# A fused attention and spectral-mixing kernel: TensorE gathers four chunks that transfers used to rearrange, and the last loop's accumulators hold the same half of two blocks

## The chip, the cores and the metric

The kernel runs on one core of one Trainium2 chip. The metric is the device time in microseconds (us) of one execution, as the median of several. Before and after, and every experiment beside the kernel before, ran on the same chip. The profiled execution has its own clock: its span, from the first to the last instruction, is about 2 us shorter than the time of the run (457.1 of 458.82 us before).

Names used below: TensorE does matrix products (PE in the profile, PEld its weight loads), VectorE (DVE) and ScalarE (ACT) do elementwise work, and SyncE (SP) here only issues transfers. SBUF is the on-chip memory; the kernel's tiles in it have up to 128 partitions. The accumulators that TensorE's products go to here are in PSUM.

## The reference

The input of the second part is the output of a causal attention, laid out as `x` with 8 batches, 576 positions and 512 channels. The change touches only the second part:

```python
# x: (8, 576, 512); w_r, w_i: (64, 512, 512); w_ch: (512, 512)      -- attention cut
X = np.fft.rfft(x, axis=1)
Xr, Xi = np.real(X[:, :64]), np.imag(X[:, :64])
Yr = einsum('bmd,mde->bme', Xr, w_r) - einsum('bmd,mde->bme', Xi, w_i)
Yi = einsum('bmd,mde->bme', Xr, w_i) + einsum('bmd,mde->bme', Xi, w_r)
y = np.fft.irfft(Yr + 1j * Yi on the first 64 modes, n=576, axis=1)
u = x + y
return u + np.maximum(u @ w_ch, 0.0)                                 # (8, 576, 512) float32
```

The weights `w_r` and `w_i` are 134 MB and are read once.

## The kernel before

The 64 modes are worked in 8 chunks of 8 modes. When the last quarter of a chunk's weights has been used, its spectrum `y` stands with mode, part and batch mixed on the partitions. The inverse transform needs modes on the partitions and batches beside each other. So each chunk is **spread**: a transfer from SBUF to SBUF rearranges 128 KB into `yv`. For the first four chunks, the product of `y` with `w_ch` is done straight from a transposed copy, eight batches one after another:

```python
def spread(c, which, rows):
    nc.sync.dma_start(out=yv[16 * c : 16 * c + 16, :, which, :], in_=rows)
# at the end of a chunk's last quarter, for every chunk c:
    spread(c, 0, yb)

def first_times_wch(b):                       # called for b in 0..7, after chunk 3
    vp = auxpool.tile([P, DM], FP32, name="v_ps", tag="aux")
    n = 2 * MC * NY                           # 64 rows
    for dt in range(DT):
        nc.tensor.matmul(
            vp[:n], yt_first[:, dt].rearrange("p c (x b) -> p (c x) b", b=B)[:, :, b],
            wch_sb[:, dt, :], start=(dt == 0), stop=(dt == DT - 1),
        )
    nc.vector.tensor_copy(out=yv[:n, b, 1, :], in_=vp[:n])
```

After the last chunk comes a loop over 18 pairs of blocks of positions. A block has 128 positions. Batches end in a short block of 64, and two of the pairs hold those. The product `x @ w_ch` of 16 pairs was made earlier, while weights were loading, and kept in SBUF in one of two **ways**. "e" keeps it as a rounded half-precision part and what the rounding lost, which a VectorE subtraction makes; TensorE puts it back into an accumulator with four products by the identity. "s" keeps it in full precision, and ScalarE copies it back. This putting back is called **seeding**:

```python
ways = dict(zip(kept, "esesessesesseses"))

def seed(i):
    ...
    if ways.get(i) == "s":
        nc.scalar.copy(out=zs[i], in_=z1s[i])
    elif ways.get(i) == "e":
        for x in range(2):
            for y in range(2):
                nc.tensor.matmul(zs[i][:, x, :], ident16h, z1s[i][:, y, x, :],
                                 start=(y == 0), stop=False, skip_group_check=True)

def start_u(i):                                # puts x into the accumulator of u = x + y
    ...
    for x, (b, T) in enumerate(pairs[i]):
        for r, bb, ident in parts(b, T):
            nc.tensor.matmul(us[i][x][r, :]..., ident, x_all[: r.stop - r.start, :, bb, T, :],
                             start=True, stop=False, ...)

def finish(i):
    ...
    for x, (b, T) in enumerate(pairs[i]):
        o = rs[i][:, x, :]
        nc.vector.tensor_tensor(out=o, in0=us[i][x], in1=o, op=ALU.add)     # u + relu(z)
        for r, bb, _ in parts(b, T):
            nc.sync.dma_start(out=out[bb, bass.ds(T * P, r.stop - r.start), :], in_=rs[i][r, x, :])

for i in range(NPRE, len(pairs)):
    pre(i)                                     # seed "e", then the inverse transform into z
    start_u(i)
    add_y(us[i], i, 0)                         # the inverse transform into u
    if ways.get(i + 1) == "s":
        seed(i + 1)
    relu(i, 2 if i == last else 1)             # ScalarE, z -> result tile
    finish(i)                                  # VectorE add, write
```

An accumulator `us[i][x]` or `zs[i][:, x]` holds one whole block, so a write of 256 KB goes to 128 consecutive rows of the output.

The softmax here doesn't subtract the row's maximum and nothing guards it: scores larger than these inputs give would overflow.

Of the kernel before, what the change touches and what calls it, by code (L numbers as in the profile page):

```python
# [9 lines left out]
FP32 = mybir.dt.float32  # L10
# [3 lines left out]
ALU = mybir.AluOpType  # L14
# [4 lines left out]
def kernel(  # L19
# [11 lines left out]
    nc = tc.nc  # L31
    B, H, S, D = q.shape
    NM = moe_w_r.shape[0]
    DM = H * D
# [40 lines left out]
    G_np[:, 0, :S] = cmv[:, None] * np.cos(ang.T)  # L75
    G_np[:, 1, :S] = -(cmv[:, None] * np.sin(ang.T))
    G_np = G_np.reshape(P, SP).astype(np.float16)

    d_ident16h = nc.inline_tensor(ident_np.astype(np.float16), name="c_ident16h").ap()
    d_ident32 = nc.inline_tensor(ident_np, name="c_ident32").ap()  # L80
# [349 lines left out]
    def modes(g, c, meanwhile=None):  # L430


        ps = auxpool.tile([P, DM], FP32, name="yp", tag="aux")
        for x in range(4):
            ri, par = divmod(x, 2)
            cols = xs[g % 2].rearrange("p k r b m -> p (k r b) m")
            c0 = (48, 16)[ri] - 16 * par
            if meanwhile and x in meanwhile:
                meanwhile[x]()
            for cg in range(4):  # L440
                nc.tensor.matmul(  # L441
                    ps[32 * cg : 32 * cg + 32, :],
                    cols[:, c0 : c0 + 32, c * MC + 2 * cg + par],
                    wt[(g, c, ri, par)][:, cg, :],
                    start=(x == 0), stop=(x == 3),
                    tile_position=(0, 32 * cg), skip_group_check=True,
                )
        if g == 0:
            nc.vector.tensor_copy(out=y_acc[:, c, :], in_=ps)
        elif g < NG - 1:  # L450
            nc.vector.tensor_tensor(out=y_acc[:, c, :], in0=ps, in1=y_acc[:, c, :], op=ALU.add)
        else:
            yb = spool.tile([P, DM], FP16, name="y_sb", tag="y")
            for cols in halves if c == NCK - 1 else [slice(0, DM)]:
                nc.vector.tensor_tensor(
                    out=yb[:, cols], in0=ps[:, cols], in1=y_acc[:, c, cols], op=ALU.add
                )
            spread(c, 0, yb)
            return yb

    halves = [slice(i * DM // 2, (i + 1) * DM // 2) for i in range(2)]
# [1 line left out]
    def spread(c, which, rows):  # L463

        nc.sync.dma_start(out=yv[16 * c : 16 * c + 16, :, which, :], in_=rows)
# [8 lines left out]
    kept = list(range(NPRE, len(pairs)))  # L474


    ways = dict(zip(kept, "esesessesesseses"))

    first_pairs = [i for i in kept[1:] if pairs[i][0][1] < NF and pairs[i][0][0] <= 4][:6]
    z1s, xts1 = {}, {}  # L480

    def kept_place(i, t):

        if ways[i] == "e":
            z1s[i] = t.bitcast(FP16).rearrange("p (y x e) -> p y x e", y=2, x=2)
        else:
            z1s[i] = t.bitcast(FP32).rearrange("p (x e) -> p x e", x=2)

    def keep_product(i, xx, z):
        if ways[i] != "e":  # L490
            nc.scalar.copy(out=z1s[i][:, xx], in_=z)
            return
        nc.scalar.copy(out=z1s[i][:, 0, xx], in_=z)
        nc.vector.tensor_tensor(out=z1s[i][:, 1, xx], in0=z, in1=z1s[i][:, 0, xx], op=ALU.subtract)
# [84 lines left out]
    def parts(b, T):  # L579
# [2 lines left out]
            return [(slice(0, P), b, ident16h)]  # L582
        return [(slice(NL * i, NL * i + NL), b + i, ident16h[:NL, :NL]) for i in range(2)]

    def x_transposed(i):
        xts[i] = xt_sb[len(xts) % 2]
        for x, (b, T) in enumerate(pairs[i]):
            ps = upool.tile([P, DT, P], FP32, name="xt_ps", tag="u")
            for rows, bb, ident in parts(b, T):
                for dt in range(DT):  # L590
                    nc.tensor.matmul(
                        ps[:, dt, rows], x_all[: rows.stop - rows.start, dt, bb, T, :],
                        ident, start=True, stop=True, skip_group_check=True,
                    )
            nc.vector.tensor_copy(out=xts[i][:, x], in_=ps)  # L595

    def x_times_wch(i, last):
        zs[i] = z = zpool.tile([P, 2, DM], FP32, name="z_ps", tag="z")
# [38 lines left out]
        spread(c, 1, vb)  # L637
        return vb

    def first_times_wch(b):  # L640
        vp = auxpool.tile([P, DM], FP32, name="v_ps", tag="aux")
        n = 2 * MC * NY
        for dt in range(DT):
            nc.tensor.matmul(
                vp[:n], yt_first[:, dt].rearrange("p c (x b) -> p (c x) b", b=B)[:, :, b],
                wch_sb[:, dt, :], start=(dt == 0), stop=(dt == DT - 1),
            )
        nc.vector.tensor_copy(out=yv[:n, b, 1, :], in_=vp[:n])


    ahead = []
# [19 lines left out]
    def add_y(dst, i, which, rows=slice(0, P), start=False):  # L671
# [4 lines that stand above are left out]
                    dst[x][r, :], G_sb[rows, bass.ds(T * P, r.stop - r.start)],  # L676
                    yv[rows, bb, which, :], start=start, stop=True, skip_group_check=True,
                    tile_position=(0, r.start),
                )
# [9 lines left out]
    def start_u(i):  # L689
        pool, tag = ((upool, "u"), (auxpool, "aux"))[i % 2]  # L690
        us[i] = [pool.tile([P, DM], FP32, name="u_ps", tag=tag) for x in range(2)]
        for x, (b, T) in enumerate(pairs[i]):
            for r, bb, ident in parts(b, T):
                nc.tensor.matmul(  # L694
                    us[i][x][r, :].rearrange("p (g d) -> p g d", d=P), ident,
                    x_all[: r.stop - r.start, :, bb, T, :],
                    start=True, stop=False, skip_group_check=True, tile_position=(0, r.start),
                )

    def result(i):  # L700

        if i % 2 == 0 or i == len(pairs) - 1:
            return finpool.tile([P, 4 * DM], BF16, name="r_sb", tag="r", bufs=3).bitcast(FP32).rearrange(
                "p (x e) -> p x e", x=2
            )
        t = wpool.tile([P, WM, DM], BF16, name="r_w", tag="w")
        return t.rearrange("p m e -> p (m e)").bitcast(FP32).rearrange("p (x e) -> p x e", x=2)

    def relu(i, parts_=1):
        rs[i] = result(i)  # L710
        for x in range(parts_):
            n = 2 // parts_
            nc.scalar.activation(
                out=rs[i][:, n * x : n * x + n], in_=zs[i][:, n * x : n * x + n], func=ACTF.Relu
            )

    def finish(i):
        if ways.get(i) == "v":
            rs[i] = result(i)
        for x, (b, T) in enumerate(pairs[i]):  # L720
            o = rs[i][:, x, :]
            if ways.get(i) == "v":
                nc.vector.tensor_tensor(out=o, in0=zs[i][:, x, :], in1=z1s[i][:, x, :], op=ALU.add)
                nc.vector.scalar_tensor_tensor(
                    out=o, in0=o, scalar=0.0, in1=us[i][x], op0=ALU.max, op1=ALU.add
                )
            else:
                nc.vector.tensor_tensor(out=o, in0=us[i][x], in1=o, op=ALU.add)
            for r, bb, _ in parts(b, T):
                nc.sync.dma_start(  # L730
                    out=out[bb, bass.ds(T * P, r.stop - r.start), :], in_=rs[i][r, x, :]
                )

    def z_of(i):
        return [zs[i][:, x, :] for x in range(2)]

    for c in range(NCK - 2):
        yb = modes(NG - 1, c)
        for x in range(TAKE[c] - 1):
            work()  # L740
        yt = y_transposed(yb, c)
        if TAKE[c]:
            work()
        if c >= NY:
            y_times_wch(c, yt)
        elif c == NY - 1:
            for b in range(B):
                first_times_wch(b)
    work()
    assert not order_z and not ahead  # L750
    c = NCK - 2
# [46 lines left out]


    def seed(i):  # L800
        if ways.get(i) in ("e", "s"):
            zs[i] = zpool.tile([P, 2, DM], FP32, name="z_ps", tag="z")
        if ways.get(i) == "s":
            nc.scalar.copy(out=zs[i], in_=z1s[i])
        elif ways.get(i) == "e":
            for x in range(2):
                for y in range(2):
                    nc.tensor.matmul(
                        zs[i][:, x, :], ident16h, z1s[i][:, y, x, :],
                        start=(y == 0), stop=False, skip_group_check=True,  # L810
                    )

    def pre(i):

        if ways[i] == "e":
            seed(i)
        elif ways[i] == "v":
            zs[i] = zpool.tile([P, 2, DM], FP32, name="z_ps", tag="z")
        add_y(z_of(i), i, 1, start=ways[i] == "v")

    if ways[NPRE] == "s":
        seed(NPRE)
# [3 lines left out]
    for i in range(NPRE, len(pairs)):  # L826
        pre(i)
        start_u(i)
        add_y(us[i], i, 0)
        if ways.get(i + 1) == "s":  # L830
            seed(i + 1)
        if ways[i] != "v":
            relu(i, 2 if i == last else 1)
        finish(i)


# [28 lines left out]
```

## Time and profile before

| | before |
|---|---|
| median of three runs | 459.39 us (458.98 to 459.42) |
| span of the profiled run | 457.1 us |
| last weight lands | about 417.7 us |
| last loop starts | 423.9 us |
| last output data | 455.3 us |

Four readings: the first two come from the page's list of transfers (out and in, engine, count, size of one, median us from issue to landing) and from the view of the output tensor (issue durations on SyncE as minimum, median and maximum in ns, then first and last start):

```profile
out_dram<-r_sb SPq DMA_DIRECT2D x16, 256.0 KB, 2.3
```

```profile
L730 SPq DMA_DIRECT2D out_dram<-r_sb x24: 332/346/597, 423.3 to 453.5; - x24
```

A write of 256 KB lands 2.3 us after its issue, and SyncE needs about a third of a microsecond to issue it. The timeline of TensorE where the first four chunks are multiplied by `w_ch` (start, duration, engine, line, operation, tiles, shape, count, and in brackets the idle time before it and what ended it):

```profile
377.18 9.01 PE L644 MATMUL v_ps<-wch_sb,yt_first 128*64 128x512 f16 x32 [0.68 <-ACT yt_first L626]
```

This is the work that the gather replaces: 9.0 us without a pause. The next lines are stretches of 4 us around it. Their columns are the stretch, its length, busy time and count of PE, PEld, DVE, ACT and POOL, the granted TensorE clock, the mean DMA share and GB/s:

```profile
378.00:382.00 4.00, 4.00 (x13) 2.45 (x12) 1.66 (x3) 0.00 (x0) 0.94 (x2) 0.67 1.23 217
382.00:386.00 4.00, 4.00 (x19) 3.28 (x17) 3.12 (x5) 0.00 (x0) 0.74 (x1) 1.00 1.24 206
```

The fourth is TensorE's timeline again, at its last group of weight products:

```profile
418.11 0.45 PE L441 MATMUL yp<-w_sb,xs 128*32 128x512 bf16 x4 [0.68 <-DMA w_sb<-in_moe_w_i_dram]
```

It idles 0.68 us until the last weights have landed.

### The profile page before, as it was taken

How to read it: one execution, taken by the hardware profiler on the slowest of the kernel's cores; microseconds unless marked ns; L12 is line 12 of the kernel's file. 1: busy time of each engine (PE TensorE's matmuls, PEld its weight loads, DVE VectorE, ACT ScalarE, POOL GpSimd, SP SyncE). 2: the span in 40 equal slices, each digit the busy share in tenths (PEclk: the TensorE clock that was granted, in tenths of full speed). 3: DMA queues.
4: the chain of work that ended last, by engine and by line, in shares of the span. 5: the costliest groups of instructions: out<-in, count | busy, mean ns of one | idle time of the engine just before them, and what ended most of it. 6: DMA issues, size and time to landing. Idle time of an engine off the chain costs nothing.

```text
span 457.1 us, 10262 instructions
## 1 busy us (share of the span) xinstructions
PE 339.1 (74%) x4177; PEld 217.2 (48%) x4209; DVE 237.3 (52%) x528; ACT 219.1 (48%) x382; POOL 182.9 (40%) x269
## 2 busy tenths in 40 slices
PE   1779968966562979936587766779967769797995
PEld 1556646644341656614355544446643326343432
DVE  7777645653242556624345544466656425442675
ACT  1587856554241747723445345446622220221895
POOL 6755555544345555344454444355423223200000
PEclk9999999998586889957778799899999778999999
DMA  9999999999999999999999999999999999995688
GB/s 177 201 203 203 202 201 204 202 204 204 204 204 201 202 202 202 204 205 204 199 192 205 204 204 204 204 203 202 207 206 212 210 210 210 214 214 105 235 285 319
DMA packets 109375, 94.54 MB, mean 207 GB/s; under 512 B 28480, under 2 KB 104512, under 8 KB 109328
## 3 DMA queue, kind: packets, MB, share of 16 engines
q0 software_dynamic: 98960, 81.81, 113.0%
q1 hardware_dynamic: 10368, 12.07, 8.5%
q8 instruction: 33, 0.54, 0.4%
q14 instruction: 14, 0.11, 0.1%
HBM read 164.56 MB, written 9.44 MB: 381 GB/s over the span
## 4 chain that ended last, share of the span: by engine, by line
DMA 70%; PE 20%; issue 4%; POOL 3%; DVE 2%; DVEq 0%; POOLq 0%
DMA w_sb<-in_moe_w_i_dram 44%; DMA q<-in_q_dram 13%; DMA w_sb<-in_moe_w_r_dram 5%; PE yp L441 3%; PE sc_ps L365 3%; PE av_ps L394 2%; DMA x_all<-in_moe_w_r_dram 2%; DMA k<-in_k_dram 2%; PE sc_ps L359 2%; DMA y_acc<-in_moe_w_i_dram 2%; PE tr_ps L324 2%; DMA y_acc<-in_moe_w_r_dram 2%; PE u_ps L694 2%; PE z_ps L675 2%; PE u_ps L675 2%
## 5 line engine op out<-in xcount | busy, mean ns | idle before, releaser
L373 ACT ACTIVATE p_sb<-sc_ps,cumt_sb 128x576 f16<-128x576 f32 (+1 forms) x256 | 141.9, 636 | 45.8 <-PE sc_ps L365 45.4
L217 POOL DMA_DIRECT2D w_sb<-in_moe_w_i_dram x60 | 45.1, 751 | 81.7 <-PE yp L441 36.8
L217 POOL DMA_DIRECT2D w_sb<-in_moe_w_r_dram x60 | 45.4, 757 | 65.2 <-DMA w_sb<-in_moe_w_r_dram 26.1
L217 POOL DMA_DIRECT2D v<-in_v_dram x72 | 50.8, 707 | 31.3 <-DMA w_sb<-in_moe_w_r_dram 8.4
L324 PE MATMUL tr_ps<-ident,q 64*64 64x64 bf16 x576 | 17.1, 208 | 55.4 <-DMA q<-in_q_dram 55.4
L359 PE MATMUL sc_ps<-negm,ident 128*128 128x256 bf16 x256 | 55.0, 300 | 0.3
L441 PE MATMUL yp<-w_sb,xs 128*32 128x512 bf16 x480 | 37.0, 408 | 22.2 <-DMA w_sb<-in_moe_w_i_dram 18.1
L327 DVE COPY qtA<-tr_ps 64x576 bf16<-64x576 bf16 x32 | 23.8, 743 | 50.8 <-PE tr_ps L324 50.7
L344 ACT ACTIVATE p<-sc_ps,cumt 128x64 f16<-128x64 f32 x32 | 10.1, 314 | 74.2 <-PE sc_ps L340 74.2
L394 PE MATMUL av_ps<-v,p_sb 128*128 128x65 f16 x1024 | 43.7, 196 | 0.0
L394 PEld LDWEIGHTS <-p_sb 128*128 128x128 f16 x1024 | 38.9, 99 | 4.8 <-issue 0.7
L327 DVE COPY ktA<-tr_ps 64x576 bf16<-64x576 bf16 x32 | 24.0, 750 | 32.7 <-PE tr_ps L324 32.7
L324 PEld LDWEIGHTS <-q 64*64 64x64 bf16 x576 | 13.3, 120 | 58.0 <-DMA q<-in_q_dram 56.9
L441 PEld LDWEIGHTS <-xs 128*32 128x32 bf16 x512 | 22.9, 169 | 32.3 <-issue 28.8
L365 PE MATMUL sc_ps<-qtB,ktB 128*128 128x64 bf16 (+2 forms) x160 | 34.8, 322 | 3.7 <-issue 2.4
L365 PE MATMUL sc_ps<-qtA,ktA 65*128 65x512 bf16 (+2 forms) x192 | 36.1, 297 | 0.3 <-DVE ktA L327 0.3
L399 DVE TENSOR_REDUCE den<-av_ps 128x5 f32<-128x10 f32 x64 | 10.8, 169 | 46.4 <-PE av_ps L394 46.4
L404 DVE TENSOR_TENSOR x_all<-av_ps,rcp 128x320 f16<-128x320 f32 x64 | 31.5, 492 | 2.2
L327 ACT COPY ktB<-tr_ps 64x576 bf16<-64x576 bf16 x32 | 20.3, 634 | 19.7 <-DVE ktA L327 18.8
L365 PEld LDWEIGHTS <-ktB 128*128 128x128 bf16 x192 | 22.4, 117 | 14.8 <-issue 6.3
L324 PE MATMUL tr_ps<-ident,k 64*64 64x64 bf16 x576 | 17.5, 210 | 14.0 <-DVE qtB L327 10.5
L601 PE MATMUL z_ps<-wch_sb,xs 128*128 128x512 f16 x96 | 26.2, 423 | 0.8 <-DVE xs L595 0.8
(112 smaller groups left out, 526.4 us busy)
## 6 DMA issues: line engine op xcount, KB each, us to landing
w_sb<-in_moe_w_r_dram POOLq DMA_DIRECT2D x60, 512.0 KB, 11.9
w_sb<-in_moe_w_i_dram POOLq DMA_DIRECT2D x60, 512.0 KB, 11.9
q<-in_q_dram POOLq DMA_DIRECT2D x32, 144.0 KB, 9.7
k<-in_k_dram POOLq DMA_DIRECT2D x32, 144.0 KB, 10.1
v<-in_v_dram POOLq DMA_DIRECT2D x72, 64.0 KB, 9.7
out_dram<-r_sb SPq DMA_DIRECT2D x16, 256.0 KB, 2.3
out_dram<-r_w SPq DMA_DIRECT2D x16, 256.0 KB, 2.6
x_all<-in_moe_w_i_dram POOLq DMA_DIRECT2D x3, 512.0 KB, 10.0
```

The lines of the kernel that those rows point to most:

```text
L217: nc.gpsimd.dma_start(out=dst, in_=src)
L324: nc.tensor.transpose(ps[rows, r, :], src[rows, r, :], ident16[rows, rows])
L327: copy(out=dst[n % NQ][rows, :].rearrange("d (p r) -> d p r", r=R), in_=ps[rows].rearrange("d r p -> d p r"),)
L359: nc.tensor.matmul(ps[:, bass.ds(w * S, W)], ident16, negm[:, bass.ts(r, W)], start=True, stop=False, skip_group_check=True,)
L365: nc.tensor.matmul(ps[:, c0 : c0 + i1 - i0], keys[:, w, r, :], qt[:, i0:i1], start=False, stop=True, skip_group_check=True,)
L373: nc.scalar.activation(out=pt[:, poff[x] : poff[x] + S - w * W], in_=ps[:, w * S : (w + 1) * S - w * W], func=ACTF.Exp, bias=cumt_sb[:, x, ...
L394: nc.tensor.matmul(ps[:, I, r : r + NCH], lhsT, rhs, start=(i == 0), stop=(i == len(todo) - 1), skip_group_check=True,)
L399: nc.vector.tensor_reduce(out=den, in_=ps[:, :, 0 : VW : NCH], axis=mybir.AxisListType.X, op=ALU.add)
L404: nc.vector.tensor_tensor(out=x_all[:, g, b, :, D * h : D * h + D], in0=ps[:, :, 1 : NCH], in1=rcp.unsqueeze(2).to_broadcast([P, NT, D]), ...
L441: nc.tensor.matmul(ps[32 * cg : 32 * cg + 32, :], cols[:, c0 : c0 + 32, c * MC + 2 * cg + par], wt[(g, c, ri, par)][:, cg, :], start=(x == ...
L601: nc.tensor.matmul(z[:, x, :], xts[i][:, x, dt, :], wch_sb[:, dt, :], start=(dt == 0), stop=(last and dt == DT - 1), skip_group_check=True,)
L675: nc.tensor.matmul(dst[x][r, :], G_sb[rows, bass.ds(T * P, r.stop - r.start)], yv[rows, bb, which, :], start=start, stop=True, skip_group_ ...
```

## The change

The intent is twofold. TensorE is idle for 112 of the first 418 us, so it can take over the rearranging of four chunks, and four spreads no longer compete with weights for the DMA engines (0.32 MB of weights came in 2 us with a spread, 0.41 in 2 us without one). In the last loop, matmuls of 64 by 64 are meant to run four at a time in the four quarters of TensorE's array, and the change lets quarters that read different partitions write different accumulators. An accumulator therefore now holds the same half of two blocks, not both halves of one: partitions 0 to 63 belong to the first block and 64 to 127 to the second. The columns of the inverse-transform matrix `G_sb` are permuted to fit. The way "e" is replaced by "f", seeded by quarters, and twelve pairs use it where seven used "e".

```diff
+    HP = P // 2
+    two = np.arange(NF * P).reshape(NF // 2, 2, 2, HP).transpose(0, 2, 1, 3).reshape(-1)
+    G_np[:, : NF * P] = G_np[:, two]
...
-            spread(c, 0, yb)
+            if c >= NCK // 2:
+                spread(c, 0, yb)
...
-    ways = dict(zip(kept, "esesessesesseses"))
+    ways = dict(zip(kept, "ffsfffffsfsffsff"))
...                                            (x_transposed: columns reordered for pairs not of way "f")
-    def first_times_wch(b):                    (body as above)
+    def gather(c0, c1):
+        n = 2 * MC * (c1 - c0)                 # 64
+        rows = slice(2 * MC * c0, 2 * MC * c1)
+        ng = P // n                            # 2
+        for b0 in range(0, B, ng):
+            vp = auxpool.tile([P, DM], FP32, name="v_ps", tag="aux")
+            yp = auxpool.tile([P, DM], FP32, name="yg_ps", tag="aux")
+            for which, ps in ((1, vp), (0, yp)):
+                for dt in range(DT):
+                    for g in range(ng):
+                        op = yt_first[:, dt, : c1 - c0].rearrange("p c (x b) -> p (c x) b", b=B)
+                        nc.tensor.matmul(
+                            ps[n * g : n * g + n, :] if which else ps[n * g : n * g + n, bass.ts(dt, P)],
+                            op[:, :, b0 + g],
+                            wch_sb[:, dt, :] if which else ident16h,
+                            ..., tile_position=(0, n * g), skip_group_check=True,
+                        )
+                for g in range(ng):
+                    dst, src = yv[rows, b0 + g, which, :], ps[n * g : n * g + n, :]
+                    if g % 2:
+                        nc.vector.tensor_copy(out=dst, in_=src)
+                    else:
+                        nc.scalar.copy(out=dst, in_=src)
...
     def start_u(i):
+        if halved(i):                          # every pair of full blocks
+            for h in range(2):
+                for x, (b, T) in enumerate(pairs[i]):
+                    own = slice(HP * h, HP * (h + 1))
+                    nc.tensor.matmul(
+                        us[i][h][HP * x : HP * (x + 1), :]..., ident16h[own, own], x_all[own, :, b, T, :],
+                        start=True, stop=False, skip_group_check=True, tile_position=(HP * h, HP * x),
+                    )
+            return
...
     def finish(i):
         for x, (b, T) in enumerate(pairs[i]):
             o = rs[i][:, x, :]
             nc.vector.tensor_tensor(out=o, in0=us[i][x], in1=o, op=ALU.add)
+            if halved(i):
+                two = out[b, bass.ds((T - x) * P, 2 * P), :]
+                nc.sync.dma_start(out=two.rearrange("(x h p) e -> h x p e", x=2, h=2)[x], in_=o)
+                continue
...
     def seed(i):
-        elif ways.get(i) == "e":
-            ...                                (four matmuls of 128x128, as above)
+        elif ways.get(i) == "f":
+            for y in range(2):
+                for h in range(2):
+                    for x in range(2):
+                        own = slice(HP * h, HP * (h + 1))
+                        nc.tensor.matmul(
+                            zs[i][HP * x : HP * (x + 1), h, :], ident16h[own, own],
+                            z1s[i][own, y, x, :], start=(y == 0), ..., tile_position=(HP * h, HP * x),
+                        )
```

The line to look at twice is the write in `finish`. Its target is two runs of 64 rows with 64 rows between them: a view of 2 by 64 by 512. The prediction has two DMA engines carry such a write. When it was made, that was the author's estimate: each of the 40 writes of the kernel before has 16 packets under 512 bytes (640 in all), and none of them has a target with fewer than 64 rows in its slowest dimension.

More of the change, by code (lines that the diff above doesn't have):

```diff
@@ L482, in kept_place @@
     def kept_place(i, t):
-        if ways[i] == "e":
+        if ways[i] == "f":
             z1s[i] = t.bitcast(FP16).rearrange("p (y x e) -> p y x e", y=2, x=2)
@@ L489, in keep_product @@
     def keep_product(i, xx, z):
-        if ways[i] != "e":
+        if ways[i] != "f":
             nc.scalar.copy(out=z1s[i][:, xx], in_=z)
@@ L583, in parts, with halved @@
         return [(slice(NL * i, NL * i + NL), b + i, ident16h[:NL, :NL]) for i in range(2)]
+    def halved(i):
+        return pairs[i][0][1] < NF
     def x_transposed(i):
@@ L594, in x_transposed @@
                     )
-            nc.vector.tensor_copy(out=xts[i][:, x], in_=ps)
+            if halved(i) and ways.get(i) != "f":
+                nc.vector.tensor_copy(
+                    out=xts[i].rearrange("p h t (x c) -> p x t h c", x=2)[:, x],
+                    in_=ps.rearrange("p t (h c) -> p t h c", h=2),
+                )
+            else:
+                nc.vector.tensor_copy(out=xts[i][:, x], in_=ps)
     def x_times_wch(i, last):
@@ L638, in y_times_wch @@
         return vb
-    def first_times_wch(b):
-        vp = auxpool.tile([P, DM], FP32, name="v_ps", tag="aux")
-        n = 2 * MC * NY
-        for dt in range(DT):
-            nc.tensor.matmul(
-                vp[:n], yt_first[:, dt].rearrange("p c (x b) -> p (c x) b", b=B)[:, :, b],
-                wch_sb[:, dt, :], start=(dt == 0), stop=(dt == DT - 1),
-            )
-        nc.vector.tensor_copy(out=yv[:n, b, 1, :], in_=vp[:n])
+    def gather(c0, c1):
[13 more added lines that the diff above has]
+                            wch_sb[:, dt, :] if which else ident16h,
+                            start=(dt == 0 or not which), stop=(dt == DT - 1 or not which),
+                            tile_position=(0, n * g), skip_group_check=True,
+                        )
[3 more added lines that the diff above has]
+                        nc.vector.tensor_copy(out=dst, in_=src)
+                    else:
+                        nc.scalar.copy(out=dst, in_=src)
     ahead = []
@@ L691, in start_u @@
         us[i] = [pool.tile([P, DM], FP32, name="u_ps", tag=tag) for x in range(2)]
+        if halved(i):
[3 more added lines that the diff above has]
+                    nc.tensor.matmul(
+                        us[i][h][HP * x : HP * (x + 1), :].rearrange("p (g d) -> p g d", d=P),
+                        ident16h[own, own], x_all[own, :, b, T, :],
+                        start=True, stop=False, skip_group_check=True, tile_position=(HP * h, HP * x),
+                    )
+            return
         for x, (b, T) in enumerate(pairs[i]):
@@ L717, in finish @@
     def finish(i):
-        if ways.get(i) == "v":
-            rs[i] = result(i)
         for x, (b, T) in enumerate(pairs[i]):
             o = rs[i][:, x, :]
-            if ways.get(i) == "v":
-                nc.vector.tensor_tensor(out=o, in0=zs[i][:, x, :], in1=z1s[i][:, x, :], op=ALU.add)
-                nc.vector.scalar_tensor_tensor(
-                    out=o, in0=o, scalar=0.0, in1=us[i][x], op0=ALU.max, op1=ALU.add
-                )
-            else:
-                nc.vector.tensor_tensor(out=o, in0=us[i][x], in1=o, op=ALU.add)
+            nc.vector.tensor_tensor(out=o, in0=us[i][x], in1=o, op=ALU.add)
+            if halved(i):
+                two = out[b, bass.ds((T - x) * P, 2 * P), :]
+                nc.sync.dma_start(out=two.rearrange("(x h p) e -> h x p e", x=2, h=2)[x], in_=o)
+                continue
             for r, bb, _ in parts(b, T):
@@ L746 @@
         elif c == NY - 1:
-            for b in range(B):
-                first_times_wch(b)
+            gather(0, NY)
     work()
@@ L800, in seed @@
     def seed(i):
-        if ways.get(i) in ("e", "s"):
+        if ways.get(i) in ("f", "s"):
             zs[i] = zpool.tile([P, 2, DM], FP32, name="z_ps", tag="z")
@@ L804, in seed @@
             nc.scalar.copy(out=zs[i], in_=z1s[i])
-        elif ways.get(i) == "e":
-            for x in range(2):
-                for y in range(2):
-                    nc.tensor.matmul(
-                        zs[i][:, x, :], ident16h, z1s[i][:, y, x, :],
-                        start=(y == 0), stop=False, skip_group_check=True,
-                    )
+        elif ways.get(i) == "f":
[5 more added lines that the diff above has]
+                            zs[i][HP * x : HP * (x + 1), h, :], ident16h[own, own],
+                            z1s[i][own, y, x, :],
+                            start=(y == 0), stop=False, skip_group_check=True,
+                            tile_position=(HP * h, HP * x),
+                        )
     def pre(i):
-        if ways[i] == "e":
+        if ways[i] == "f":
             seed(i)
-        elif ways[i] == "v":
-            zs[i] = zpool.tile([P, 2, DM], FP32, name="z_ps", tag="z")
-        add_y(z_of(i), i, 1, start=ways[i] == "v")
+        add_y(z_of(i), i, 1)
     if ways[NPRE] == "s":
@@ L831 @@
             seed(i + 1)
-        if ways[i] != "v":
-            relu(i, 2 if i == last else 1)
+        relu(i, 2 if i == last else 1)
         finish(i)
```

## The prediction

> **What bounds the kernel now.** I read the page's slices first, then the chain of waits, then the last 40 us by stretches, by timeline and by DMA view.
>
> The slices, and the chain's line:
>
> ```profile
> DMA  9999999999999999999999999999999999995688
> GB/s 177 201 203 203 202 201 204 202 204 204 204 204 201 202 202 202 204 205 204 199 192 205 204 204 204 204 203 202 207 206 212 210 210 210 214 214 105 235 285 319
> DMA 70%; PE 20%; issue 4%; POOL 3%; DVE 2%; DVEq 0%; POOLq 0%
> ```
>
> Until about 416 us the DMA engines are full; 70% of the chain is transfers, mostly weights. So nothing that the change does to TensorE, VectorE or ScalarE before that moment counts, as long as the weights keep coming; only bytes taken off the DMA engines do. The last weight lands at 418.1 us. Then comes a tail of 39 us, which stretches show like this:
>
> ```profile
> core 0: us, PE busy (x) PEld busy (x) DVE busy (x) ACT busy (x) POOL busy (x), PEclk, DMA share, GB/s
> 418.10:424.00 5.90, 5.18 (x35) 2.92 (x35) 2.92 (x7) 2.68 (x6) 0.00 (x0) 1.00 0.16 44
> 423.90:452.00 28.10, 28.09 (x137) 11.52 (x135) 20.12 (x32) 24.74 (x27) 0.00 (x0) 1.00 0.84 297
> ```
>
> The last loop runs from 423.9 to 452.0. TensorE is busy for all of it and is its bound; ScalarE is at 24.7 of 28.1 us, the output writes at 0.84 of the DMA engines. Writes are therefore close behind. The timeline of one iteration of the cheap-on-ScalarE kind ("e": four seed matmuls) and the pair of short tiles behind it:
>
> ```profile
> 427.36 1.03 PE L808 MATMUL z_ps<-r_sb,ident16h 128*128 128x512 f16 x4
> 428.31 0.62 PE L675 MATMUL z_ps<-yv,G_sb 128*64 128x512 f16 x4
> 428.87 0.62 PE L694 MATMUL u_ps<-x_all,ident16h 64*64 64x512 f16 x4
> 429.42 0.62 PE L675 MATMUL u_ps<-yv,G_sb 128*64 128x512 f16 x4
> 429.97 0.60 PE L675 MATMUL z_ps<-yv,G_sb 128*128 128x512 f16 x2
> 430.41 0.59 PE L694 MATMUL u_ps<-x_all,ident16h 128*128 128x512 f16 x2
> ```
>
> Read the starts, not the durations. Two full-array matmuls take 430.41 - 429.97 = 0.43 us, so 0.216 us each. Four on half the columns take 0.55 us: they run in two concurrent twos (2 x 0.216 = 0.43), and about 0.12 is left for changing the array's division.
>
> The output writes, in the DMA view of 423.6 to 457 us and of the full stretch 446 to 455 us:
>
> ```profile
> DMA packets 5251, 9.47 MB, mean 284 GB/s; under 512 B 640, under 2 KB 640, under 8 KB 5248
> ```
>
> ```profile
> DMA packets 1877, 3.43 MB, mean 381 GB/s; under 512 B 208, under 2 KB 208, under 8 KB 1876
> q1 hardware_dynamic: 1876, 3.42, 98.9%
> ```
>
> The 40 output transfers have 4608 packets of 2 KB and 640 tiny ones, 16 completion writes for each: all 16 engines work on every transfer. In the stretch 448 to 452 us the writes run at 406 GB/s with the engines full: 25.4 GB/s for an engine, 80.7 ns for a packet of 2 KB.
>
> [...]
>
> **The change part by part.**
>
> *Spreads.* Four transfers of 128 KB (first four chunks of y) go. The DMA view of 388 to 390 us, without a spread, has 0.41 MB of weights; 392 to 394 us, with one, has 0.32. A spread takes 0.09 MB of weights' room: 0.44 us at 205 GB/s. Four are 1.8 us, and the weights are the chain: the last lands at 416.3.
>
> *Gather.* Line 644's 32 matmuls of N=512 took 9.0 us from 377 us on one column half. Now they run in twos on both halves, with 32 matmuls of N=128 and 16 copies of 64x512 on two engines through two PSUM buffers; I estimate 8 us. TensorE waits for weights 1.9 us at 395.6 and 1.2 us at 415.1, so this is hidden: 0.
>
> *Seeds and accumulators in the tail.* With 0.216 us for a slot and 0.11 us (estimate, between 0.09 from single starts and 0.12) for a change of division:
> - before: 7 "e" of 10 slots (2.16), 7 "s" of 6 slots (1.30), 2 short pairs (1.66 from the timeline): 27.5 us, observed 28.1.
> - after: 12 "f", each 8 quarter seeds in fours (2 slots), 4 quarter matmuls of x (1), 4 full (4), 4 changes: 1.51 + 0.44 = 1.95; 2 "s" of 5 slots and 2 changes: 1.30; 2 short pairs 1.66: 29.3 us.
>
> The quarters save three slots in an "f" against an "e" and lose 0.44 us of it to changes, and five pairs move from the 6-slot kind to "f". TensorE gets 1.8 us more. ScalarE loses 5 seeds of 1.02 us; it wasn't the bound. Five more subtractions on VectorE lie before 416 us: 0.
>
> So compute and spreads cancel: 459.4 - 1.8 + 1.8 = 459.4.
>
> *Output writes.* Here I expect the result to be decided. With the same half of two blocks in a tile, a write's target is no longer 128 rows in a row but two blocks of 64. The changed program's listing has 32 writes of 2x64x512 (before: 128x512) and 8 of 64x512 unchanged. The slowest dimension of the target is 2[...]. Each engine then has 64 packets of 2 KB a write: 64 x 80.7 ns = 5.16 us. 32 writes are 165.3 us; the 8 short ones add 4 packets each, 2.6 us: 167.9 us of work one after another on two engines, against 28 us for the loop. Output begins at about 422.3 (before, data flowed from 424.1; less 1.8). 422.3 + 167.9 = 590.2; the end follows the last byte by 1.8 us as before (data ended at 455.3, the span at 457.1): 592.0. The timed runs are 2.3 us above the span: 594.
>
> **Rivals.**
> - *All 16 engines carry the writes anyway* (the dimension is divided somewhere on the way to the chip). For it: the change looks tuned, and nobody would keep a loss of 130 us. Against it: the listing is what is built[...]. Time: 459, within 455 to 463.
> - *TensorE's changes of division bound the tail*: true only if the first rival is; then each 0.05 us per change is 2.5 us.
> - *The four quarters don't overlap*: then an "f" has 8 + 4 quarters in twos, 3 slots more, some 8 us in all: 467, again only if writes stay spread.
> - *Two engines, but another rate.* With fewer competitors a packet could reach the 76.9 ns of the best half-microsecond before (426 GB/s): 586.[...]
>
> **Range and chances.** I give the two-engine mechanism 0.86; within it 572 to 635 covers the rates. The rest is nearly all within 2%, as spreads and changes of division are each below 3 us.
>
> **What would show it.** Right: in the tail the DMA share falls to about 2/16 with some 50 GB/s for 165 us; tiny packets of the output fall from 640 to 192 (32 x 2 + 8 x 16); landing times of the outputs grow from 2.3 us to over 5; the chain ends in output transfers, and TensorE waits for accumulators or result tiles. Last weight near 416.3; steps of "f" near 1.95 us where nothing holds them. Wrong: 128 KB writes still at some 400 GB/s; then the tail's TensorE steps decide, and the time is near 459.

## The result, and the profile after

| | before | after |
|---|---|---|
| median | 459.19 us (458.70 to 459.65, 6 runs) | 597.99 us (596.84 to 600.96, 6 runs) |
| ratio | | 1.303, 95% interval 1.2999 to 1.3062 |
| span of the profiled run | 457.1 us | 595.1 us |
| last weight lands | 417.7 us | 415.0 us |
| last loop starts | 423.9 us | 425.15 us |
| first and last output data | 424.1 to 455.3 us | 425.66 to 593.75 us |

The ratio is the mean time of one kernel's fast runs over the mean of the other's fast runs of the same rounds, so it is not quite the ratio of the medians. The same holds for every ratio below. The change costs 139 us.

The page of the changed kernel, with the slices now of 14.9 us each and the line of the chain:

```profile
DMA  9999999999999999999999999999111211211111
GB/s 187 201 203 202 202 203 204 204 204 201 201 203 204 204 203 195 204 204 204 205 203 204 207 207 206 206 209 175 42 52 57 77 51 51 82 51 52 51 51 47
DMA 63%; PE 15%; issue 4%; DVE 3%; SPq 2%; POOL 2%; ACT 2%; DVEq 0%; ACTq 0%; POOLq 0%
```

Where the slices of before end in 235, 285 and 319 GB/s, these run on for twelve slices, most of them at about 50 GB/s, with the DMA engines at one or two tenths. Transfers are 63% of the longer chain, 0.63 x 595.1 = 375 us, where they were 0.70 x 457.1 = 320 us. SyncE's issuing queue (SPq) has entered it too. The DMA view of 421 to 595 us, its totals and the queue of the writes:

```profile
DMA packets 5092, 9.75 MB, mean 56 GB/s; under 512 B 224, under 2 KB 480, under 8 KB 5088
q1 hardware_dynamic: 5088, 9.70, 15.5%
```

Of the 224 packets under 512 bytes, two late spreads account for 32. That leaves 192 for the 40 output writes. Before, it was 640. The number 192 is 32 x 2 + 8 x 16: in the trace's list of packets these have 4 bytes and close a write, two for each of the 32 with the split target, on the plateau 5.13 us from pair to pair, and 16 for each of the eight short ones, as for every write before. Two packets of the writes' queue are under way at a time for 147.0 of the 168.1 us in which output flows; before, it was 16 or more for 19.9 of 31.2 us. So two engines carry a write with the split target. The queue's share is 15.5%, against 98.9% in the full stretch before. In the plateau from 525 to 570 us, where long writes alone run, the DMA view gives 13.1% at 51 GB/s: close to 2/16 = 12.5%, and 25.5 GB/s for each of two engines. The output's data flows from 425.66 to 593.75 us, which is 168.1 us.

The output tensor's view, in the same columns as before:

```profile
L763 SPq DMA_DIRECT2D out_dram<-r_sb x16: 528/4949/7107, 424.4 to 575.7; - x16
```

The issue of a write now takes 4.95 us of SyncE's time in the median, not a third of one. That is nearly the time of one write on two engines (64 packets of 80.8 ns are 5.17 us). The issuing doesn't set this pace: in SyncE's timeline the first two issues, from 424.43 us, take 1.26 us together, the next two 8.36 us. Each of the two engines moves 25.5 GB/s, as much as each of sixteen moved before when they were full (406 GB/s from 448 to 452 us, 25.4 for each). So SyncE is held by the writes before it. The waits of 424 to 595 us (who waited for whom, total us, times, longest):

```profile
DVE r_sb L760 <- ACT r_sb L753: 94.7, 9, 18.7
ACT r_sb L753 <- DMA out_dram<-r_sb: 94.4, 7, 19.4
PE z_ps L846 <- ACT r_sb L753: 35.6, 3, 15.8
```

This is how a slow write reaches TensorE. ScalarE waits for result tiles (`r_sb`) whose writes haven't ended; VectorE and TensorE wait for ScalarE. No compute engine is slow in itself. One iteration of the kind "f", before the queue of writes has filled, is this in TensorE's timeline:

```profile
425.15 0.63 PE L846 MATMUL z_ps<-r_sb,ident16h 64*64 64x512 f16 x8
425.71 0.61 PE L705 MATMUL z_ps<-yv,G_sb 128*128 128x512 f16 x2
426.24 0.41 PE L726 MATMUL u_ps<-x_all,ident16h 64*64 64x512 f16 x4
426.58 0.61 PE L705 MATMUL u_ps<-yv,G_sb 128*128 128x512 f16 x2
427.12 0.63 PE L846 MATMUL z_ps<-z,ident16h 64*64 64x512 f16 x8
```

The step is 427.12 - 425.15 = 1.97 us. The eight quarter seeds take 0.56 us: two slots of 0.216 us and 0.13 us around them, so four quarters do run at once.

Two places differ before the last loop. TensorE's timeline at the gather and later:

```profile
375.03 1.98 PE L666 MATMUL v_ps<-wch_sb,yt_first 128*64 128x512 f16 x8 [0.68 <-ACT yt_first L640]
376.80 0.65 PE L666 MATMUL yg_ps<-ident16h,yt_first 128*64 128x128 f16 x8
378.41 1.98 PE L666 MATMUL v_ps<-wch_sb,yt_first 128*64 128x512 f16 x8 [0.96 <-DVE yv L676]
...
388.53 1.96 PE L445 MATMUL yp<-w_sb,xs 128*32 128x512 bf16 x16 [0.95 <-DVE yv L676]
...
407.40 1.90 PE L615 MATMUL z_ps<-wch_sb,xs 128*128 128x512 f16 x8 [3.11 <-DVE xs L604]
```

The gather takes from 375.03 to 388.53 us, 13.5 us where before needed 9.0. Four times TensorE waits about 0.95 us for a VectorE copy out of the PSUM buffer: three times in front of the next `v_ps` group, and once in front of the weight product that follows. The stretch of 382 to 386 us, in the columns of the stretches before:

```profile
382.00:386.00 4.00, 3.05 (x21) 2.35 (x20) 1.64 (x3) 1.06 (x2) 0.00 (x0) 0.50 1.24 206
```

The clock is at 0.50, where before it was back at 1.00, and TensorE is busy for 3.05 of 4 us. The last line of the timeline shows another wait, 3.11 us for a VectorE cast (`xs`); the kernel before waits 0.56 us at this place (404.69 us). And at the end of the weights TensorE does not wait any more:

```profile
419.21 0.47 PE L445 MATMUL yp<-w_sb,xs 128*32 128x512 bf16 x4
```

The last weights landed at 415.0 us, but their product starts at 419.21 us, with TensorE busy without a gap before it. TensorE is late there, and its earlier waits are the visible reason; an experiment below divides them.

### The profile page after: what moved, and what is told of

Its sections match the earlier page's. It is cut to its first block, busy times and chain, and to the rows that moved or that the text cites. A ratio compares the mean times of both kernels' runs of the same rounds, so it can differ in the third digit from the quotient of the medians.

```text
span 595.1 us, 10559 instructions
## 1 busy us (share of the span) xinstructions
PE 359.1 (60%) x4341; PEld 217.9 (37%) x4341; DVE 242.6 (41%) x537; ACT 218.4 (37%) x385; POOL 183.0 (31%) x269
## 4 chain that ended last, share of the span: by engine, by line
DMA 63%; PE 15%; issue 4%; DVE 3%; SPq 2%; POOL 2%; ACT 2%; DVEq 0%; ACTq 0%; POOLq 0%
DMA w_sb<-in_moe_w_i_dram 18%; DMA out_dram<-r_sb 15%; DMA w_sb<-in_moe_w_r_dram 13%; DMA q<-in_q_dram 12%; PE yp L445 2%; PE z_ps L615 2%; PE sc_ps L369 2%; DMA x_all<-in_moe_w_r_dram 2%; SPq L763 1%; PE sc_ps L363 1%; PE v_ps L666 1%; DMA y_acc<-in_moe_w_i_dram 1%; DMA y_acc<-in_moe_w_r_dram 1%; PE tr_ps L328 1%; SPq L766 1%
## 5 line engine op out<-in xcount | busy, mean ns | idle before, releaser
L363 PE MATMUL sc_ps<-negm,ident 128*128 128x256 bf16 x256 | 56.9, 309 | 0.2
L760 DVE TENSOR_TENSOR r_sb<-u_ps,r_sb 128x512 f32<-128x512 f32 x20 | 12.9, 686 | 95.5 <-ACT r_sb L753 94.7
L753 ACT ACTIVATE r_sb<-z_ps 128x1024 f32<-128x1024 f32 (+1 forms) x12 | 10.4, 880 | 98.7 <-DMA out_dram<-r_sb 94.4
L398 PE MATMUL av_ps<-v,p_sb 128*128 128x65 f16 x1024 | 45.2, 199 | 0.0
L369 PE MATMUL sc_ps<-qtB,ktB 128*128 128x512 bf16 (+2 forms) x192 | 44.7, 351 | 0.0
L398 PEld LDWEIGHTS <-p_sb 128*128 128x128 f16 x1024 | 40.2, 101 | 5.1 <-issue 1.2
L369 PE MATMUL sc_ps<-qtA,ktA 65*128 65x512 bf16 (+2 forms) x192 | 38.0, 309 | 0.4 <-DMA qtA<-ncum_sb 0.4
```

Source lines behind the costliest of these rows:

```text
L363: nc.tensor.matmul(ps[:, bass.ds(w * S, W)], ident16, negm[:, bass.ts(r, W)], start=True, stop=False, skip_group_check=True,)
L369: nc.tensor.matmul(ps[:, c0 : c0 + i1 - i0], keys[:, w, r, :], qt[:, i0:i1], start=False, stop=True, skip_group_check=True,)
L398: nc.tensor.matmul(ps[:, I, r : r + NCH], lhsT, rhs, start=(i == 0), stop=(i == len(todo) - 1), skip_group_check=True,)
```

## The experiments

Four theories were to be told apart. **Two engines**: the shape of the write's target leaves 14 engines out, and nothing else matters much. **Gaps**: the cost comes from a target that isn't consecutive. **TensorE**: the quarters or the gather cost time by themselves. **Queue**: SyncE's issuing is the limit. Ten kernels ran. Those called wrong put right values into wrong rows; their instructions and bytes are what is measured.

### blocks_2, blocks_4, blocks_16: the kernel before with only the write's target divided

The kernel before is unchanged but for `finish`. The 128 rows go to g groups of 128/g rows with gaps of the same size between them. The rows are wrong, as the accumulators hold whole blocks.

```diff
+            if T < NF:
+                two = out[b, bass.ds((T - x) * P, 2 * P), :]
+                nc.sync.dma_start(out=two.rearrange("(g y r) e -> y g r e", g=2, y=2)[x], in_=o)   # g = 2, 4, 16
+                continue
```

> Kernel before, only the 32 long output writes take the form of the changed kernel (target 2x64 rows instead of 128; rows land in the wrong place on purpose). Theory 'two engines' (slowest dimension of the target sets how many DMA engines carry a write): 32 writes x 64 packets x 80 ns after 424 us, so 592 to 598 us, DMA share in the tail 2/16, tiny completion packets of the outputs 192. Rival 'TensorE and accumulators' (the quarters or the shared accumulators hold up the tail): 459 us, as nothing of them is here. Rival 'gaps' (a target in separate blocks is slow to write): slow, 550 to 600.

> As blocks_2, target 4x32 rows (wrong rows on purpose). 'Two engines' theory: four engines, 32 x 32 packets x 80 ns = 82 us + 2.6, so 424 + 84.5 + 4 = 511 to 517 us, tail at 100 to 105 GB/s. 'TensorE and accumulators': 459. 'Gaps': as slow as blocks_2 or slower, since the blocks are smaller.

> As blocks_2, target 16x8 rows (wrong rows on purpose): the most gaps, but a slowest dimension of 16. 'Two engines' theory: all 16 engines, 459 us within 1%, 640 completion packets. 'Gaps': slowest of the three, over 590 us.

| groups | median | ratio, 95% interval |
|---|---|---|
| 2 | 596.38 us (595.90 to 596.86, 2 runs) | 1.2992 (1.2958 to 1.3025) |
| 4 | 516.93 us (516.01 to 517.84, 2 runs) | 1.1261 (1.1225 to 1.1296) |
| 16 | 461.80 us (460.67 to 463.38, 4 runs) | 1.0058 (1.0024 to 1.0092) |

The DMA views, totals and the writes' queue. First two groups, from 424 to 590 us:

```profile
DMA packets 4770, 9.33 MB, mean 56 GB/s; under 512 B 206, under 2 KB 246, under 8 KB 4767
q1 hardware_dynamic: 4767, 9.30, 15.5%
```

Four groups, from 424 to 512 us:

```profile
DMA packets 4933, 9.45 MB, mean 107 GB/s; under 512 B 268, under 2 KB 396, under 8 KB 4930
q1 hardware_dynamic: 4930, 9.42, 31.6%
```

Sixteen groups, from 423.6 to 460 us:

```profile
DMA packets 5395, 9.60 MB, mean 264 GB/s; under 512 B 656, under 2 KB 784, under 8 KB 5392
q1 hardware_dynamic: 5392, 9.57, 82.3%
```

All three land in their expected range. The bytes are the same within 3%. The tiny packets follow 32 x g + 8 x 16: 192, 256 and 640, and 12 to 16 more, about as many as one spread at the edge of the stretch has. The rate doubles from two groups to four. Sixteen groups have the most gaps and are within 1% of before, so "gaps" falls as the main cause. One line of one write, put into the kernel before, makes 137 of the 139 us, and with it neither gather nor quarters are there: "TensorE" falls as the main cause.

### plain_writes: the changed kernel with consecutive targets

This is the opposite test: everything of the change stays but the target. The rows are wrong.

```diff
             if halved(i):
-                two = out[b, bass.ds((T - x) * P, 2 * P), :]
-                nc.sync.dma_start(out=two.rearrange("(x h p) e -> h x p e", x=2, h=2)[x], in_=o)
+                nc.sync.dma_start(out=out[b, bass.ds(T * P, P), :], in_=o)
                 continue
```

> Changed kernel, but each long write goes to 128 consecutive rows, as before (rows land in the wrong place on purpose): all of the change except the form of its writes. Theory: the tail begins at 425.3 us and is TensorE's (last matmul at 454.5 as in whole_blocks), and the writes follow 3.7 us behind as before: 461.5 to 463 us, +0.6%. Rival (something else of the halved accumulators costs, as the 467 of whole_blocks might say): 465 or more.

Measured: 464.16 us (462.20 to 465.69, 4 runs), ratio 1.0106 (1.0069 to 1.0142). The form of the write is worth 597.99 - 464.16 = 133.8 us of the 138.8. The other 5.0 us belong to the rest of the change. That is more than was expected: the time lies above the range of 461.5 to 463 and just below the rival's 465. In the profiled run the clock stayed at 0.50 from 378 to 394 us, the last loop starts at 428.0 us, 4.1 us later than in the kernel before, and TensorE is busy without a break from there to 457.3 us: 29.3 us, as computed, and 1.2 more than the 28.1 before. Start and loop together are about these 5 us. The start isn't the same in every execution: in the changed kernel's own profile, with the clock at 0.74 from 390 to 394 us, the loop began at 425.15 us.

### whole_blocks: the changed kernel, right results, targets on 16 engines

A pair's two blocks are both finished after the second addition. Then the source can be the 64 partitions of a block with its two halves, and the target 64 rows by 2. The slowest dimension is 64 on both sides. In the profile these writes have 640 packets under 512 bytes again (672 from 420 to 465 us, less 32 of two spreads), and the DMA engines are at 0.84.

```diff
-            if halved(i):
-                two = ...; nc.sync.dma_start(out=two.rearrange(...)[x], in_=o)
-                continue
+            if halved(i):
+                continue
+        if halved(i):
+            for x, (b, T) in enumerate(pairs[i]):
+                nc.sync.dma_start(
+                    out=out[b, bass.ds(T * P, P), :].rearrange("(h p) e -> p h e", h=2),
+                    in_=rs[i][HP * x : HP * (x + 1), :, :],
+                )
```

> Changed kernel, right result, output written block by block after both adds: 64 partitions x 2 halves x 2 KB, slowest dimension 64, still 32 writes of 256 KB. 'Two engines' theory: 16 engines again; the tail is then TensorE's, 12 steps of 1.97 us + 2 of 1.3 + 2 of 1.66 from 425.2 us, so 460 to 464 us. 'TensorE and accumulators': stays over 560 us.

Measured: 467.23 us (466.45 to 470.70, 4 runs), ratio 1.0193 (1.0150 to 1.0235), results right. So a repair within the change takes back 131 us, but it missed its range from above. TensorE's loop is as computed, from 425.26 to 454.75 us, 29.5 us. The output's data, however, ends only at 463.4 us. The stretch of the writes, in the columns of the stretches: first the kernel before, then this one.

```profile
424.20:455.30 31.10, 27.88 (x136) 11.34 (x134) 21.40 (x34) 24.87 (x26) 0.00 (x0) 1.00 0.85 304
```

```profile
427.00:463.00 36.00, 27.91 (x218) 7.01 (x216) 20.62 (x32) 19.77 (x21) 0.00 (x0) 0.92 0.84 258
```

The DMA engines are equally full, 0.85 and 0.84, but move 304 GB/s in the one and 258 GB/s in the other. The mean write packet of 2 KB takes 90 ns before and 106 ns here. The median is 84 ns in both; the mean rises because 26% of the packets take over 130 ns, where it was 9%. Equally full engines at a lower rate: the writes of this form cost more for each packet. blocks_16 has the same mark in a milder form, 101 ns and 20%; its issues take 0.55 us in the median, where it was 0.33. whole_blocks changed both ends of the write, a source of 64 partitions and a target of two alternating runs of rows; which of them does it wasn't separated.

### two_queues: is it the issuing of whole_blocks that limits it?

SyncE's issues in whole_blocks take 0.62 to 0.71 us in the median, twice those of before. If that were the limit, a second queue would help.

```diff
-                nc.sync.dma_start(
+                (nc.sync, nc.gpsimd)[x].dma_start(
```

> whole_blocks with every second long write issued from GpSimd's queue. In whole_blocks TensorE ended at 454.7 us but one queue issued writes back to back (0.75 us each) until 460.8. Theory 'issue bound': the end follows TensorE again, 461 to 463 us. Rival 'transfers bound' (writes from 64 partitions run slower: mean packet 106 ns against 90): 465 to 468, no gain.

Measured: 466.12 us (465.80 to 468.77, 4 runs), ratio 1.0163 (1.0138 to 1.0188). The intervals of the two kernels overlap. A stretch in its loop, in the columns of the stretches:

```profile
440.00:448.00 8.00, 8.00 (x67) 2.07 (x60) 6.20 (x10) 6.24 (x7) 2.19 (x4) 1.00 0.86 280
```

The engines are at 0.86 and the rate at 280 GB/s. A 2 KB packet of SyncE's queue takes 105 ns; GpSimd's queue carries packets of 4 KB, which take 203 ns. So "queue" falls here: the transfers themselves limit. Why packets of 64-partition writes, or of 16 groups of rows, take longer is not settled.

### whole_blocks_spread: the late start of the last loop, gather or ways?

TensorE's loop in whole_blocks starts 1.4 us later than in the kernel before although the weights end earlier. One theory blames the slow gather; the rival blames the new ways with their additional subtractions. Here the gather is undone in whole_blocks: `spread(c, 0, yb)` for every chunk, and `first_times_wch(b)` for eight batches.

> whole_blocks without the gather (first chunks spread as before): the halved accumulators and the new choice of ways alone. Theory: the extra VectorE subtractions make TensorE wait 3.1 us at 404 us, which alone fits into its slack, so the tail begins near 424 us, 1.2 us earlier than in whole_blocks (425.3), and ends with the writes as there: 465 to 466.5 us. Rival (the ways alone delay the tail): 467 or more.

Measured: 466.83 us (465.58 to 468.39, 4 runs), ratio 1.0167 (1.0144 to 1.0191). The loop starts at 425.42 us and the last weight product at 419.5 us. Its TensorE timeline has these two lines:

```profile
406.08 2.77 PE L614 MATMUL z_ps<-wch_sb,xs 128*128 128x512 f16 x8 [3.11 <-DVE xs L603]
419.49 0.47 PE L445 MATMUL yp<-w_sb,xs 128*32 128x512 bf16 x4
```

Without the gather the lateness is still all there, and so is the wait of 3.11 us for the VectorE cast. The time itself doesn't decide: it lies between the theory's 465 to 466.5 and the rival's 467. The start of the loop does, and there the rival is right: the ways delay, not the gather. gather_alone, next, is the other half of the test: with the gather and without the new ways the wait at this place is 0.56 us and the last weight product starts at 416.74 us. The halved accumulators are in whole_blocks_spread too; plain_few_quarters, which has them with only seven "f", waits 1.16 us at this place and starts that product at 416.75 us.

### gather_alone and gather_four_banks: the gather in the kernel before

The first takes only the gather and the four dropped spreads into the kernel before. The second, on top of that, lets the gathered `y` use another pair of PSUM buffers, so that the two products alternate over four buffers and not over two:

```diff
-            yp = auxpool.tile([P, DM], FP32, name="yg_ps", tag="aux")
+            yp = upool.tile([P, DM], FP32, name="yg_ps", tag="u")
```

> Kernel before plus the gather alone (four spreads go, tail untouched). In the changed kernel the gather took 13.5 us of TensorE's time line (9.0 before) and the last weights landed at 415.0 us (417.8 before). Theory 'slack': TensorE had 3.8 us of waits for weights between 395 and 418 us; the 2.4 us by which the gather ends later fit in, so the tail begins 1 to 2 us earlier: 457 to 458.5 us. Rival 'gather costs what it gains': tail begins as before or later, 459 to 461.

> As gather_alone, but the y part of the gather goes through the two idle u banks, so no matmul waits for a copy (four waits of 0.95 us in the changed kernel). Theory 'slack': gather near 9.5 us, tail begins with the last weights, 2 to 2.8 us earlier than before: 456 to 457.5 us, the best of all. Rival (spreads were free): 459.

Measured: gather_alone 457.32 us (456.53 to 458.10, 6 runs), ratio 0.9960 (0.9945 to 0.9975); gather_four_banks 456.84 us (456.38 to 457.34, 5 runs), ratio 0.9950 (0.9934 to 0.9966). Results are right in both, and both times lie in their expected ranges. With two buffers the gather takes 13.5 us, at a clock of 0.50 from 378 to 390 us, as in the changed kernel, and still the last weights land at 416.07 us and the loop starts at 422.55 us, 1.35 us earlier than before. The timeline of TensorE with four buffers:

```profile
375.88 1.98 PE L653 MATMUL v_ps<-wch_sb,yt_first 128*64 128x512 f16 x8 [0.68 <-ACT yt_first L627]
377.66 0.65 PE L653 MATMUL yg_ps<-ident16h,yt_first 128*64 128x128 f16 x8
378.10 1.74 PE L653 MATMUL v_ps<-wch_sb,yt_first 128*64 128x512 f16 x8
...
382.86 1.12 PE L441 MATMUL yp<-w_sb,xs 128*32 128x512 bf16 x16
```

The waits between the groups are gone, and the gather takes 382.86 - 375.88 = 7.0 us. The stretch of 382 to 386 us:

```profile
382.00:386.00 4.00, 3.78 (x44) 2.46 (x41) 3.93 (x7) 1.34 (x3) 0.75 (x2) 1.00 1.24 206
```

The clock is back at 1.00. The 6.5 us saved in the gather are worth 0.5 us in the medians, and the two intervals overlap: they lie beside the weights. gather_four_banks has the lowest time of the kernels with right results; it beats the kernels before and after, the former by 0.5%, with an interval that excludes 1.

### plain_few_quarters: fewer pairs by quarters

Seven pairs by quarters and nine by ScalarE, as in the kernel before, with plain_writes' targets (wrong) and the gather over four buffers: would the quarters then gain?

```diff
-    ways = dict(zip(kept, "ffsfffffsfsffsff"))
+    ways = dict(zip(kept, "fssfsfsfsfsfsfss"))
```

> As plain_writes (wrong rows on purpose), with 7 pairs seeded by quarters in place of 12 (ScalarE seeds the others, as before) and the gather through four banks: does the TensorE part of the change gain anything if no write is in the way? Theory: loop of 7 x 1.97 + 7 x 1.32 + 2 x 1.66 = 26.4 us against 28.1, from about 421.9: 454.5 to 456.5 us. Rival (ScalarE or the writes bound the loop as soon as TensorE is quicker): 456.5 to 458, no better than gather_four_banks.

Measured: 456.35 us (455.91 to 456.92, 4 runs), ratio 0.9936 (0.9907 to 0.9965). The time lies just inside the theory's range, but the ratio also lies within the interval of gather_four_banks, 0.9934 to 0.9966, as the rival said. TensorE's loop does shorten to 26.4 us, from 422.67 to 449.1 us. But data of the output flows until 453.64 us, and the DMA engines run at 400 GB/s in much of it. The loop also starts 0.8 us later than in gather_four_banks (421.87 us). What TensorE saves in the loop is not seen in the time. ScalarE is busy for 24.4 of these 26.5 us and appears in the chain too, so the writes need not be the only limit; the two weren't separated.

## Why the prediction was right, and where its steps were off

**Right: the mechanism and its size.** Two engines carry each of the 32 writes: two packets under 512 bytes for each, and 51 GB/s at a DMA share of 13.1% on the plateau. That the split target would bring this was an estimate when it was made; the runs show it. The prediction's signs all came: 192 tiny packets, about 51 GB/s, landings of over 5 us (the pieces of the chain that wait for a write's landing are 8.3 to 20.4 us long), the chain in output transfers, TensorE waiting for result tiles through ScalarE. Its sign for "wrong" names writes of 128 KB, where 256 KB was meant. Its term "167.9 us of work one after another on two engines" measured 168.1 us, that is 80.8 ns for each of 2080 packets on an engine, where 80.7 was used. The series of two, four and sixteen groups shows that the count of groups sets the rate (56, 107 and 264 GB/s), and plain_writes shows by removal that the form of the write is the cause.

**Right: TensorE's steps.** An "f" was put at 1.95 us and took 1.97. The loop was put at 29.3 us, and where writes leave it alone it took 29.5 (whole_blocks) and 29.3 (plain_writes). The estimate of 0.11 us for a change of division fits: in the step of 1.97 us, 7 slots of 0.216 us leave 0.46 us for four changes, 0.10 to 0.13 us for each by the starts; before, two full matmuls with no change behind them took 0.43 us. A slip in the working had no effect: one of the seven "e" of before is a short pair, so six full pairs moved to "f", not five. The four seed slots are counted once either way, and the sum of 27.5 us stands.

**Off by 3.4 us: the start of the output.** "Output begins at about 422.3" was 425.7. The prediction's sum is 594.3 before rounding. The profiled run took 596.84 us, 2.5 more: the late start, less 0.8 us in the other terms together. The median of the six runs lies 1.15 us above the profiled one; that part isn't broken down. Two steps bear on the start.

- *"Five more subtractions on VectorE lie before 416 us: 0."* This step failed. An "f", like an "e", needs a ScalarE copy and then a VectorE subtraction of 1.23 us, and more of them now stand in front of casts that TensorE waits for. TensorE's wait at 407.4 us is 3.11 us, where it was 0.56, and from then on it runs behind the weights. The last weights landed at 415.0 us, earlier than the predicted 416.3 (which took the start of the last product, 418.1 us, for the landing at 417.7), but their product came at 419.2 us, later than in the kernel before (418.1). whole_blocks_spread shows the delay with the gather undone. That work "lies before" the last weight was true; that it was therefore free was not.
- *"I estimate 8 us ... so this is hidden: 0."* The gather's size was wrong: 13.5 us, as waits for two PSUM buffers came four times and the clock stayed at 0.50. That it is hidden was nearly right: gather_four_banks takes 7.0 us and its median is only 0.5 us lower. The step's zero survived although its 8 us didn't: that was luck, as TensorE had nearly enough slack there.

**"So compute and spreads cancel: 459.4"** is the sum of these. With the writes made plain the changed kernel takes 464.2 us. The part on spreads held: four spreads were put at 1.8 us of weights' time, and gather_alone's last weights land 1.6 us earlier than before (416.07 and 417.7 us), with 1.8 us gained in the median.

So the gain that the change aimed at in the weight phase exists and is about 2 us, in gather_four_banks. The quarters with twelve "f" pairs more than give it back: plain_writes is 5.0 us above the kernel before. The write costs 134 us on top.

**Open:** why writes on all 16 engines from 64 partitions, or to 16 groups of rows, have longer packets; and whether the writes or ScalarE hold plain_few_quarters. For the changed accumulators, no split into four or more groups was run; the series was run on the kernel before only.

## What to carry to other kernels

When a change rearranges what lies on the partitions of a result, look first at the view that its write then has: in these runs its slowest dimension set how many DMA engines carried it (2 groups moved 56 GB/s in the mean, 4 moved 107, 16 moved 264), and 2 instead of 128 cost 134 us while every engine's arithmetic stayed near its plan. Count the packets under 512 bytes to see it; here a write had 2, 4 or 16 of them with 2, 4 or 16 groups. Here, work beside a long load was free only while the engine that consumes the load still waited for it: the gather's 13.5 us, where 9.0 were before, did not keep the last loop from starting 1.35 us earlier in gather_alone, while the new ways made TensorE wait 3.11 us for a cast and begin the last weight product at 419.5 us in whole_blocks_spread, where it was 418.1; ask for each new operation there whom it stands in front of.
